# Lightning attention with a balanced expert layer: eight routing steps with the experts run beside them

## The chip, the core and the metric

One core of a Trainium2 chip runs the kernel alone. Its engines are TensorE (PE in the profile, with its weight loads listed apart as PEld), VectorE (DVE), ScalarE (ACT), GpSimd (POOL) and SyncE (SP). Each has its own queue of instructions and works through it in order; they wait for each other through semaphores. DMA transfers are issued from the queues of SP, ACT and POOL. The metric is the device time of one execution in microseconds, as the median of several runs. One execution was also profiled; every duration below is from it.

## What is computed

The input is a decayed linear attention over 4 batches, 8 heads, 768 positions and head size 64, in blocks of 64 positions:

```python
for b in range(nb):
    intra = np.einsum('bhic,bhjc->bhij', qb, kb) * Dmask[None]
    intra = np.einsum('bhij,bhjd->bhid', intra, vb)
    inter = np.einsum('bhid,bhde->bhie', qb * lam_pow[None], kv_state)
    out[:, :, sl] = intra + inter
    kv_state = lam_block[...] * kv_state + np.einsum('bhsd,bhse->bhde', kb_dec, vb)
```

Its output, seen as 3072 tokens of 512 numbers, goes through a layer of 8 experts. Every expert takes exactly 384 tokens. All 3072 x 8 scores are sorted, and the pairs are handed out from the best down:

```python
logits = x @ w_gate
order = np.argsort(-logits.flatten())
for idx in order:
    tok, e = (int(idx) // E, int(idx) % E)
    if assigned[tok] >= 0 or counts[e] >= cap:
        continue
    assigned[tok] = e
    counts[e] += 1
for e in range(E):
    mask = assigned == e
    out[mask] = np.maximum(x[mask] @ w1[e], 0.0) @ w2[e]
```

The assignment can be had without a sort. As long as no expert is full, every token goes to its best expert. At some score the first expert becomes full. From there on each remaining token's best choice is among the experts left, until the next one is full, and so on: eight fillings, each with one threshold.

## The kernel before

**Attention** (lines 146 to 286). For each batch, every head's q, k and v (192 KB each) are loaded, scaled, split into a high and a low bf16 part, and transposed on PE. Then six blocks of 128 positions follow, each over eight heads. The outputs are cast into `x_sb` (L285) and the gate scores into `logits_sb` (L286); one 3 MB transfer (L288) writes x to `x_dram` after the last batch.

**Weights** (L298, L300). All sixteen expert matrices are loaded by POOL's queue, from fp32 to bf16, right after attention. They take 16 buffers, so nothing depends on the routing.

**Routing.** Twelve rounds of a search for the first threshold (L345 to L358): DVE compares all scores with three candidates, reduces, and PE adds over the partitions. Tokens above the threshold are assigned. The rest are compacted to at most 640 rows by 120 one-hot matrices of 128x128 in fp32 (L426, L428). Seven phases (from L446) then fill the remaining experts: each takes every row's best open expert, sends the keys by a small DMA to one partition (L466), spreads them by PE (L468), ranks all against all (L473, L476), finds the worst score that still fits, and updates the state. After the last phase the assignment is scattered (L542), read back, turned into target positions, and a list of tokens by expert is scattered with 24 indirect DMAs (L587).

**Experts** (from L597), 0 to 7 in the order of their numbers. For each: load its token list `permt`, gather its 384 rows by three indirect DMAs `xe` (L606), transpose twelve tiles (L613) which ACT copies out one by one (L614), 32 matmuls with `w1t` (L619), relu on ACT (L621), 24 matmuls with `w2t` (L625), a copy on DVE (L628), and three indirect DMAs that scatter the rows to the output (L629). Their order by time follows a scheduler that places instructions into the queues by its own estimate of when they can run; what depends on nothing moves ahead.

What touches the change: `x_sb` and L288, everything from L298 to L587, and the expert loop.

Of the kernel before, what the change touches and what calls it, by code (L numbers as in the profile page):

```python
# [8 lines left out]

FP32 = mybir.dt.float32  # L10
BF16 = mybir.dt.bfloat16
I32 = mybir.dt.int32
AX = mybir.AxisListType
OP = mybir.AluOpType
# [3 lines left out]

# [3 lines left out]
def _PBF(a, lead):  # L22
    newap = [[0, lead[0]]] + [[0, r] for r in lead[1:]] + [list(x) for x in a.ap[1:]]
    return _dc.replace(a, ap=newap)


def _PBS(a, shape):
    newap = [[0, shape[0]]] + [[0, r] for r in shape[1:]]
    return _dc.replace(a, ap=newap)


@with_exitstack
def kernel(
# [11 lines left out]
    nc = tc.nc  # L45
    P = 128
# [5 lines left out]
    FF = 1024  # L52
    CAP = N // E
    NCHUNK = N // P
    NC = 5
    NEG = -64.0
# [3 lines left out]
    persist = ctx.enter_context(tc.tile_pool(name="persist", bufs=1))  # L60
    actx = ExitStack()
# [13 lines left out]

    slt = const.tile([P, P], BF16)
    nc.gpsimd.memset(slt, 0.0)
    nc.gpsimd.affine_select(
        out=slt, in_=slt, compare_op=OP.is_ge, fill=1.0, base=0,
        pattern=[[-1, P]], channel_multiplier=1,  # L80
    )

    ident = const.tile([P, P], FP32)
    make_identity(nc, ident)
    identb = const.tile([P, P], BF16)
    make_identity(nc, identb)

    ones_col = const.tile([P, 1], FP32)
    nc.vector.memset(ones_col, 1.0)
    ones128 = const.tile([P, P], FP32)  # L90
    nc.vector.memset(ones128, 1.0)
    ones_1 = const.tile([1, P], FP32)
    nc.vector.memset(ones_1, 1.0)

# [4 lines left out]

    iota_e_i = const.tile([P, E], I32)  # L100
    nc.gpsimd.iota(iota_e_i, pattern=[[1, E]], base=0, channel_multiplier=0)
    iota_e = const.tile([P, E], FP32)
    nc.vector.tensor_copy(iota_e, iota_e_i)
    iota3_i = const.tile([P, 3], I32)
    nc.gpsimd.iota(iota3_i, pattern=[[1, 3]], base=1, channel_multiplier=0)
    iota3 = const.tile([P, 3], FP32)
    nc.vector.tensor_copy(iota3, iota3_i)
    iotaU_i = const.tile([P, P], I32)
    nc.gpsimd.iota(iotaU_i, pattern=[[1, P]], base=0, channel_multiplier=0)
    iotaU = const.tile([P, P], FP32)  # L110
    nc.vector.tensor_copy(iotaU, iotaU_i)

    tok_i = const.tile([P, NCHUNK], I32)
    nc.gpsimd.iota(tok_i, pattern=[[P, NCHUNK]], base=0, channel_multiplier=1)
    row_i = const.tile([P, NCHUNK], I32)
    nc.gpsimd.iota(row_i, pattern=[[1, NCHUNK]], base=0, channel_multiplier=NCHUNK)
    row_f = const.tile([P, NCHUNK], FP32)
    nc.vector.tensor_copy(row_f, row_i)


# [16 lines left out]

    x_sb = persist.tile([P, NCHUNK, DM], BF16)
    logits_sb = persist.tile([P, NCHUNK, E], FP32)

    x_dram = dram.tile([N, DM], BF16)
    cdram = dram.tile([NC * P, 16], FP32)
    perm_dram = dram.tile([N, 1], I32)
    asgn_dram = dram.tile([N, 1], FP32)

    for b in range(B):
# [92 lines left out]
        for t in range(NB):  # L239
# [45 lines left out]
            nc.scalar.copy(x_sb[:, oc, :], po)  # L285
# [5 lines left out]
    wpre = ctx.enter_context(tc.tile_pool(name="wpre", bufs=1))  # L291
    w1r = moe_w1.rearrange("e (ko p) f -> e p ko f", p=P)
    w2r = moe_w2.rearrange("e (ko p) f -> e p ko f", p=P)
    w1ts = []
    w2ts = []
    for e in range(E):
        w1t = wpre.tile([P, 4, FF], BF16, tag=f"w1t{e}")
        nc.gpsimd.dma_start(out=w1t, in_=w1r[e])  # L298
        w2t = wpre.tile([P, 8, DM], BF16, tag=f"w2t{e}")
        nc.gpsimd.dma_start(out=w2t, in_=w2r[e])  # L300
        w1ts.append(w1t)
        w2ts.append(w2t)

    bctx = ExitStack()
    ap = bctx.enter_context(tc.tile_pool(name="ap", bufs=1))
    app = bctx.enter_context(tc.tile_pool(name="app", bufs=2))
    apps = bctx.enter_context(tc.tile_pool(name="apps", bufs=2, space=bass.MemoryType.PSUM))

    assigned = ap.tile([P, NCHUNK], FP32)
    nc.vector.memset(assigned, -1.0)  # L310
    counts = ap.tile([P, E], FP32)
    nc.vector.memset(counts, 0.0)
    capt = ap.tile([P, E], FP32)
    nc.vector.memset(capt, float(CAP))

    val0 = ap.tile([P, NCHUNK], FP32)
    nc.vector.reduce_max(val0, logits_sb, axis=AX.X)
    bsel0 = ap.tile([P, NCHUNK, E], FP32)
    nc.vector.tensor_tensor(bsel0, logits_sb, val0[:, :, None].to_broadcast([P, NCHUNK, E]),
                            OP.is_equal)  # L320
    cand0 = ap.tile([P, E, NCHUNK], FP32)
    c0v = cand0.rearrange("p e c -> p c e")
    nc.vector.tensor_tensor(c0v, logits_sb, bsel0, OP.mult)
    bm0 = ap.tile([P, NCHUNK, E], FP32)
    nc.vector.tensor_scalar(bm0, bsel0, 1.0, -NEG, OP.subtract, OP.mult)
    nc.vector.tensor_tensor(c0v, c0v, bm0, OP.add)

    npart = app.tile([P, E], FP32, tag="npart")
    nc.vector.reduce_sum(npart, bsel0.rearrange("p c e -> p e c"), axis=AX.X)
    nps = apps.tile([P, E], FP32, tag="aps1")  # L330
    nc.tensor.matmul(nps, ones128, npart, start=True, stop=True)
    ne = ap.tile([P, E], FP32)
    nc.vector.tensor_copy(ne, nps)

    lo = ap.tile([P, E], FP32)
    nc.vector.memset(lo, -0.625)
    mid = ap.tile([P, 3, E], FP32)
    step = 0.3125
    nc.vector.scalar_tensor_tensor(
        mid, iota3[:, :, None].to_broadcast([P, 3, E]), step,  # L340
        lo[:, None, :].to_broadcast([P, 3, E]), OP.mult, OP.add)
    capt3 = capt[:, None, :].to_broadcast([P, 3, E])
    for it in range(12):
        ge = app.tile([P, 3, E, NCHUNK], FP32, tag="ge")
        nc.vector.tensor_tensor(ge, cand0[:, None, :, :].to_broadcast([P, 3, E, NCHUNK]),  # L345
                                mid[:, :, :, None].to_broadcast([P, 3, E, NCHUNK]), OP.is_ge)
        gred = app.tile([P, 3, E], FP32, tag="gred")
        nc.vector.reduce_sum(gred, ge, axis=AX.X)
        cps = apps.tile([P, 3 * E], FP32, tag="aps1")
        nc.tensor.matmul(cps, ones128, gred.rearrange("p i e -> p (i e)"),  # L350
                         start=True, stop=True)
        sel = app.tile([P, 3, E], FP32, tag="sel")
        nc.vector.tensor_tensor(sel, cps.rearrange("p (i e) -> p i e", e=E), capt3, OP.is_ge)
        svec = app.tile([P, E], FP32, tag="svec")
        nc.vector.reduce_sum(svec, sel.rearrange("p i e -> p e i"), axis=AX.X)
        nc.vector.scalar_tensor_tensor(lo, svec, step, lo, OP.mult, OP.add)
# [305 lines left out]
```

## Time and profile before

| | us |
|---|---|
| median of 3 runs | 870.17 |
| fastest and slowest run | 861.41, 871.03 |
| profiled execution, first to last instruction | 862.5 |
| attention in it, up to | 393 |
| last w2 matmul of the last expert starts its block at | 845.82 |

The page gives no other time for the profiled execution than its span. On the page a row of a group says: line, engine, operation, what it writes and reads with the tile names (buffer numbers left out), the shape, how often; then the busy time of all, the mean of one in ns; then the engine's idle time ahead of them and what ended it. A row of the timeline says: start, duration, engine, line, operation, tiles, count, and in brackets the idle time ahead of it. A row of stretches is explained where it is shown. The granted clock is the share of its full clock at which PE was let run.

### The profile page before, as it was taken

The page shows a single profiled execution, that of the slowest core. Times are in us where ns is not written, and L with a number is a line of the kernel's source. Part 1 is how long each engine was busy: PE and PEld are TensorE (multiplying, and loading weights), DVE is VectorE, ACT ScalarE, POOL GpSimd, SP SyncE. Part 2 cuts the span into 40 slices and gives each one's busy share as a digit, 9 for nine tenths or more (in the row PEclk, how much of TensorE's full clock was granted, in tenths as well). Part 3 has the DMA queues.
Part 4 walks back from the last instruction along what each step waited for, and adds up shares of the span by engine and source line. Part 5 has one row for each costly group of instructions (what it writes and reads, how often), then busy time and mean ns, then how long its engine had stood idle before and what let it go on. Part 6 is the DMA issues. An engine that isn't in the chain of part 4 may idle for free. (4 is left out here: it accounts for less than half of the span.)

```text
span 862.5 us, 12438 instructions
## 1 busy us (share of the span) xinstructions
PE 544.2 (63%) x4353; PEld 452.3 (52%) x4353; DVE 416.8 (48%) x1722; ACT 208.1 (24%) x571; POOL 296.2 (34%) x679
## 2 busy tenths in 40 slices
PE   2799968997799978993169932232210003978774
PEld 1689957997689957993169921111100001434332
DVE  6754486545854477446665677667721000110101
ACT  4552245323542245220000000000000001444331
POOL 6822495228913496324110000000022333233342
PEclk9995556655555558555555555555555555988988
DMA  8400162005400170007999500000000001122121
GB/s 147 94 19 2 33 142 48 2 2 111 102 11 1 26 141 20 2 1 197 209 210 209 103 1 0 1 0 1 1 1 0 0 0 37 48 75 80 56 86 62
DMA packets 98078, 49.12 MB, mean 57 GB/s; under 512 B 80352, under 2 KB 91616, under 8 KB 98016
## 3 DMA queue, kind: packets, MB, share of 16 engines
q0 software_dynamic: 16544, 26.24, 14.2%
q1 hardware_dynamic: 56240, 15.80, 8.6%
q10 hardware_dynamic: 25232, 6.31, 3.4%
q8 instruction: 34, 0.56, 0.3%
q14 instruction: 28, 0.23, 0.1%
HBM read 55.62 MB, written 9.46 MB: 75 GB/s over the span
## 5 line engine op out<-in xcount | busy, mean ns | idle before, releaser
L614 ACT COPY xeT<-pt 128x128 bf16<-128x128 bf16 x96 | 18.4, 285 | 380.2 <-PE pt L613 379.6
L276 PE MATMUL pkv<-vgf,ksq 128*128 128x8 f32 x384 | 107.4, 354 | 0.0
L628 DVE COPY oe<-ph 128x512 f32<-128x512 f32 x24 | 16.6, 691 | 185.3 <-PE ph L625 146.6
L267 PE MATMUL pg<-vgf,sTm 128*128 128x8 f32 x384 | 104.9, 347 | 0.5 <-DVE sTm L257 0.5
L276 PEld LDWEIGHTS pkv<-vgf,ksq 128*128 128x128 f32 x384 | 98.8, 316 | 0.0
L267 PEld LDWEIGHTS pg<-vgf,sTm 128*128 128x128 f32 x384 | 94.9, 305 | 1.1 <-DVE sTm L257 0.8
L279 DVE TENSOR_TENSOR kvb_h<-kvb_h,pkv 64x64 bf16<-64x64 bf16 x192 | 40.8, 213 | 108.5 <-PE pkv L276 108.1
L281 POOL CAST kvg_h<-wg_acc 64x8 bf16<-64x8 f32 x192 | 37.9, 197 | 145.3 <-DVE lacc L271 77.2
L259 ACT CAST sTh<-sTm 128x128 bf16<-128x128 f32 x192 | 53.5, 298 | 113.6 <-DVE sTm L257 102.1
L613 PE MATMUL pt<-identb,xe 128*128 128x128 bf16 x96 | 11.2, 239 | 97.4 <-DMA xe<-x_dram,permt 95.5
L542 POOL DMA_INDIRECT asgn_dram<-asgc,tokci x5 | 5.0, 1001 | 189.4 <-DVE logc L530 183.7
L257 DVE TENSOR_TENSOR sTm<-ps,tri 128x128 f32<-128x128 f32 x192 | 52.2, 279 | 18.6 <-PE ps L254 15.4
L613 PEld LDWEIGHTS <-xe 128*128 128x128 bf16 x96 | 6.4, 104 | 104.0 <-issue 80.5
L428 PE MATMUL psC<-pay,pch 128*128 128x12 f32 x240 | 59.2, 373 | 2.5 <-DVE pch L426 2.5
L428 PEld LDWEIGHTS psC<-pay,pch 128*128 128x128 f32 x240 | 55.7, 311 | 6.1 <-DVE pch L426 2.6
L254 PE MATMUL ps<-TCh,TBh 128*128 128x128 bf16 x192 | 57.2, 301 | 0.0
L253 PE MATMUL ps<-TAh,TBh 128*128 128x128 bf16 x192 | 50.3, 265 | 7.3 <-ACT TBh L203 6.2
L619 PE MATMUL ph<-xeT,w1t 128*128 128x384 bf16 x256 | 54.3, 372 | 1.0 <-ACT xeT L614 0.9
L268 PEld LDWEIGHTS <-TAh 128*128 128x128 bf16 x192 | 53.1, 276 | 0.0
L274 PE MATMUL pkv<-vt,kt 128*128 128x64 bf16 x192 | 46.2, 241 | 7.8 <-DVE wg_acc L280 7.8
L426 DVE TENSOR_TENSOR pch<-pos,iou 128x128 f32<-128x128 f32 x120 | 35.0, 292 | 23.6 <-PE psC L428 16.0
L282 POOL TENSOR_TENSOR kvg_h<-wg_acc,kvg_h 64x8 bf16<-64x8 f32 x192 | 39.6, 206 | 14.9 <-POOL kvg_h L281 0.2
(233 smaller groups left out, 1468.5 us busy)
## 6 DMA issues: line engine op xcount, KB each, us to landing
w1t<-in_moe_w_dram POOLq DMA_DIRECT2D x8, 1024.0 KB
w2t<-in_moe_w_dram POOLq DMA_DIRECT2D x8, 1024.0 KB
vf<-in_v_dram ACTq DMA_DIRECT2D x32, 192.0 KB, 3.1
ksq<-in_q_dram SPq DMA_DIRECT2D x32, 192.0 KB, 3.6
kf<-in_k_dram SPq DMA_DIRECT2D x32, 192.0 KB, 2.9
x_dram<-x_sb SPq DMA_DIRECT2D x1, 3072.0 KB, 16.6
perm_dram<-tok_i,desti POOLq DMA_INDIRECT x24
xe<-x_dram,permt POOLq DMA_INDIRECT x24
```

Of the source, the lines that this page charges most:

```text
L253: nc.tensor.matmul(ps, TB, TA, start=True, stop=False)
L254: nc.tensor.matmul(ps, TB, TC, start=False, stop=True)
L257: nc.vector.tensor_tensor(sTm, ps, tri, OP.mult)
L259: nc.scalar.copy(sTh, sTm)
L267: nc.tensor.matmul(pg, sTm, vgf[:, t, :], start=True, stop=False)
L268: nc.tensor.matmul(pg, TA, kvg[h][:, 0, :], start=False, stop=False)
L274: nc.tensor.matmul(pkv[:, 0:D], kt[:, t, :, :], vt[:, t, 0, :], start=True, stop=False)
L276: nc.tensor.matmul(pkv[:, D : D + E], ksqs[h][:, t, :, :], vgf[:, t, :], start=False, stop=True)
L279: nc.vector.tensor_tensor(kvb[h][0:64], kvb[h][0:64], pkv[0:64, 0:D], OP.add)
L282: nc.gpsimd.tensor_tensor(kvg[h][0:64, 1, :], wgacc[h], kvg[h][0:64, 0, :], OP.subtract)
L428: nc.tensor.matmul(psC[:, uc, :], pch, pay[:, tci, :], start=(tci == 0), stop=(tci == NCHUNK - 1))
L619: nc.tensor.matmul(ph1, w1t[:, kc, fc * P : (fc + 1) * P], xeT[:, kc, :], start=(kc == 0), stop=(kc == 3))
```

## The change

Attention stays as it is but for its output: each block of 128 tokens is written to `x_dram` as soon as it is there, by 24 transfers on SP's queue.

Routing is new. `phase1` finds the first threshold with three counts instead of a search. A score is written as a number of three digits of seven bits each. For one digit, a one-hot-like matrix `ind` (is the token's digit at least k, for k = 0 to 127) is the stationary operand and the one-hot of the token's best expert the moving one; 24 bf16 matmuls give, for every k and every expert, how many tokens reach it. PE and a maximum turn this into the digit at which the first expert holds 384. After three digits the threshold is known. The tokens of every expert above it get slots by a prefix sum, and one more product gives the token list `perm` of the full expert. The rest of the tokens (at most 640) are compacted into 5 columns with keys `Z`.

`phase(i)` does the same for the remaining rows, with 5 matmuls per digit, and returns the list of the i-th expert to become full, and that expert's number. The eighth phase takes what is left and needs no count.

The experts run in the order in which they become full. After a phase, POOL reads the expert's number into a register, issues the loads of that expert's two matrices (three buffers now, where there were eight), and the gathers. Phase i + 1 is written ahead of expert i, so the scheduler may put them side by side. The copy of the output is now on ACT, and one copy takes four transposed tiles.

A flag collects the cases that this way can't handle: two equal scores of a token's best, more than 640 tokens left, counts that don't come out at 384. All engines read it at the end; if it is set, `_exact_path` does the whole routing over by bisection, with loops, and runs all experts again. Counting with the reference's own inputs, 260 tokens are left after the first filling.

The core of the diff, with the new functions:

```diff
+    def phase1(self, ctx, L):
...
+        def count(zq, onesm):
+            ind = sp.tile([P, P, 24], BF16, tag="ind", bufs=2)
+            cps = ps.tile([P, 8], F32, tag="cnt")
+            for hh in range(2):
+                ts = slice(hh * 12, hh * 12 + 12)
+                nc.vector.tensor_tensor(ind[:, :, ts], zq[:, None, ts].to_broadcast([P, P, 12]),
+                                        self.i_kt[:, :, ts], OP.is_ge)
+                for t in range(hh * 12, hh * 12 + 12):
+                    nc.tensor.matmul(cps, ind[:, :, t], ohb[:, t, :], start=(t == 0),
+                                     stop=(t == 23))
+            S = sp.tile([P, 8], BF16, tag="S", bufs=2)
+            nc.vector.tensor_scalar(S, cps, 384.0, None, OP.is_ge)
+            nps = ps.tile([P, 8], F32, tag="n")
+            nc.tensor.matmul(nps, onesm, S, start=True, stop=True)
+            nm = sp.tile([P, 1], F32, tag="nm", bufs=2)
+            nc.vector.reduce_max(nm, nps, axis=AX.X)
+            return nps, nm
...
+        for t in range(24):
+            nc.tensor.matmul(pe1, A[:, :, t], B1v[:, :, :, t], start=(t == 0), stop=(t == 23))
...
+        yield perm, eidx
...
+        for j in range(5):
+            nc.vector.tensor_tensor(
+                R[:, 87 + 24 * j : 87 + 24 * j + 24, :],
+                R[:, 58 + j : 59 + j, :].to_broadcast([P, 24, 24]),
+                Ls.rearrange("p s e t -> p (s e) t"), OP.mult)
+        psC = ps.tile([P, 207], F32, tag="pos")
+        for t in range(24):
+            nc.tensor.matmul(psC, A[:, :, t], R[:, :, t], start=(t == 0), stop=(t == 23))
...
+    def phase(self, i):
...
+            for r in range(3):
+                ind = sp.tile([P, 5, P], BF16, tag="indc")
+                cps = ps.tile([P, 8], F32, tag="cnt")
+                for c in range(5):
+                    nc.vector.tensor_scalar(ind[:, c, :], self.kio[r], zr[:, c : c + 1], None,
+                                            OP.is_le)
+                    nc.tensor.matmul(cps, ind[:, c, :], oh[:, c, :], start=(c == 0), stop=(c == 4))
+                S = sp.tile([P, 8], BF16, tag="Sc")
+                nc.vector.tensor_tensor(S, cps, self.big, OP.is_ge)
+                nps = ps.tile([P, 8], F32, tag="n")
+                nc.tensor.matmul(nps, self.ones[r], S, start=True, stop=True)
...
+        for c in range(5):
+            nc.vector.tensor_scalar(A5[:, c, :], self.kio1, kb[:, c : c + 1], None,
+                                    OP.is_equal)
+            nc.tensor.matmul(pe, A5[:, c, :], Bv[:, :, :, c], start=(c == 0), stop=(c == 4))
...
+class _Moe:
...
+        self.wp = ctx.enter_context(tc.tile_pool(name="mw", bufs=3))
...
+    def weights(self, eidx):
+        nc, P = self.nc, 128
+        ev = nc.values_load(eidx, engines=[mybir.EngineType.Pool], min_val=0, max_val=7)
+        return self.weights_at(ev)
+
+    def weights_at(self, ev):
+        nc, P = self.nc, 128
+        w1t = self.wp.tile([P, 4, 1024], BF16, tag="w1t")
+        nc.gpsimd.dma_start(out=w1t, in_=self.w1r[bass.ds(ev, 1)].rearrange("o p k f -> p (o k) f"))
+        w2t = self.wp.tile([P, 8, 512], BF16, tag="w2t")
+        nc.gpsimd.dma_start(out=w2t, in_=self.w2r[bass.ds(ev, 1)].rearrange("o p k f -> p (o k) f"))
+        return w1t, w2t
...
+            oe = self.mp.tile([P, 512], F32, tag="oe", bufs=4)
+            nc.scalar.copy(oe, p2)
+            nc.gpsimd.indirect_dma_start(
+                out=self.out, out_offset=bass.IndirectOffsetOnAxis(ap=perm[:, c : c + 1], axis=0),
+                in_=oe, in_offset=None, bounds_check=3071, oob_is_err=False)
...
+def _route_and_moe(ctx, tc, L, router, moe):
+    gen = router.phase1(ctx, L)
+    perm, eidx = next(gen)
+    xe = moe.gather(perm)
+    w1t, w2t = moe.weights(eidx)
+    for _ in gen:
+        pass
+    for i in range(8):
+        if i < 7:
+            nperm, neidx = router.phase(i + 1)
+            nxe = moe.gather(nperm)
+            nw = moe.weights(neidx)
+        moe.ffn(perm, xe, w1t, w2t)
+        if i < 7:
+            perm, xe, (w1t, w2t) = nperm, nxe, nw
+    return router.flag()
+
+def _check_and_mend(ctx, tc, L, router, moe, dram, fi):
+    fv = tc.nc.values_load(fi, min_val=0, max_val=1)
+    with tc.If(fv > 0):
+        with ExitStack() as fctx:
+            _exact_path(fctx, tc, L, router, moe, dram)
...
-            nc.scalar.copy(x_sb[:, oc, :], po)
+            xs = work.tile([P, DM], BF16, tag="xs")
+            nc.scalar.copy(xs, po)
+            nc.sync.dma_start(out=x_dram[oc * P : (oc + 1) * P, :], in_=xs)
             nc.gpsimd.tensor_copy(logits_sb[:, oc, :], lacc)
-
-    nc.sync.dma_start(out=x_dram.rearrange("(c p) d -> p c d", p=P), in_=x_sb)
     actx.close()
...
-    for e in range(E):
-        w1t = wpre.tile([P, 4, FF], BF16, tag=f"w1t{e}")
-        nc.gpsimd.dma_start(out=w1t, in_=w1r[e])
-        w2t = wpre.tile([P, 8, DM], BF16, tag=f"w2t{e}")
-        nc.gpsimd.dma_start(out=w2t, in_=w2r[e])
...
-    for ph in range(7):
...
+    moe = _Moe(ctx, tc, identb, x_dram, moe_w1, moe_w2, out)
+    fi = _route_and_moe(ctx, tc, logits_sb, router, moe)
+    _check_and_mend(ctx, tc, logits_sb, router, moe, dram, fi)
```

How the scheduler lays this out, at two places. First PE, between two experts. Before, an expert is transposes and then its w1 matmuls, with nothing between (`xe` the gathered rows, `pt` their transposes, `ph` the first product):

```order
L613 LDWEIGHTS xe
L613 MATMUL pt<-identb,xe 128x128
L613 LDWEIGHTS xe
L613 MATMUL pt<-identb,xe 128x128
L619 LDWEIGHTS w1t
L619 MATMUL ph_8580<-xeT,w1t 128x384
```

In the new kernel, at the start of the expert after the second one: the last matmul of a count (`cps`, from the indicators `ind` and the one-hots `oh`), a tile's four transposes, and then the matmul that turns the count into a digit (`nps`, from `S`).

```order
L330 LDWEIGHTS ind
L330 MATMUL cps<-oh,ind 128x8
L483 LDWEIGHTS xe
L483 MATMUL pt<-identb,xe 128x128
L483 LDWEIGHTS xe
L483 MATMUL pt<-identb,xe 128x128
L483 LDWEIGHTS xe
L483 MATMUL pt<-identb,xe 128x128
L483 LDWEIGHTS xe
L483 MATMUL pt<-identb,xe 128x128
L334 LDWEIGHTS ones_95
L334 MATMUL nps<-S,ones_95 128x8
```

The three counts of the next phase now stand between this expert's transposes and its first w1 matmuls; the later products of the phase stand between w1 matmuls, and the 24 w2 matmuls stay in one piece.

Second POOL. Before, its queue in the expert stage holds gathers and scatters alone, after the two scatters of the routing:

```order
L542 DMA asgn_dram<-asgc,tokci 3072x1 x5
L587 DMA perm_dram<-tok_i,desti 3072x1 x24
L606 DMA xe<-x_dram,permt 128x512 x6
L629 DMA out_dram<-oe,permt 3072x512 x3
L606 DMA xe<-x_dram,permt 128x512 x3
```

In the new kernel a step is the read of the expert's number (`ei`), the two weight loads, the gathers with the new list, and the scatters of the expert before:

```order
L466 TENSOR_LOAD ei
L466 ISA x2
L472 ISA
L472 DMA w1t<-in_moe_w_dram 128x4x1024
L474 ISA
L474 DMA w2t<-in_moe_w_dram 128x8x512
L458 DMA xe<-x_dram,perm 128x512 x3
L500 DMA out_dram<-oe,perm 3072x512 x3
```

So the weights moved from ahead of the routing to the middle of each step, and each scatter of an expert now stands between the gathers of one phase and the register read of the next.

More of the change, by code (lines that the diff above doesn't have):

```diff
@@ L60 @@
     persist = ctx.enter_context(tc.tile_pool(name="persist", bufs=1))
+    ident = const.tile([P, P], FP32)
+    make_identity(nc, ident)
+    identb = const.tile([P, P], BF16)
+    make_identity(nc, identb)
+    router = _Router(ctx, tc, ident, identb)
+    logits_sb = persist.tile([P, NCHUNK, E], FP32)
+    x_dram = dram.tile([N, DM], BF16)
     actx = ExitStack()
@@ L98 @@
     nc.vector.tensor_copy(n_idx, n_idx_i)
[L100 to L118, printed above, removed]
     lam_sb = const.tile([P, E], FP32)
@@ L136 @@
     nc.vector.tensor_tensor(wg_lo[0:64], wgf, wg_hi[0:64], OP.subtract)
[L138 to L144, printed above, removed]
     for b in range(B):
@@ L307 @@
[L307 to L356, printed above, removed]
-        step = step * 0.25
-        nc.vector.scalar_tensor_tensor(
-            mid, iota3[:, :, None].to_broadcast([P, 3, E]), step,
-            lo[:, None, :].to_broadcast([P, 3, E]), OP.mult, OP.add)
```

858 lines of the change are left out of this document (561 added, 297 removed).

## The prediction

> **What bounds the kernel now.** I read first the busy time by stretches, with the stage borders taken from the timeline, then the groups by line, then the timeline at the borders. (The page's chain of waits holds only the last three pieces and says nothing of the stages.) Columns: stretch in us, length, busy time and instructions of PE, PE's weight loads, DVE, ACT, POOL, granted clock, DMA share, GB/s.
>
> ```profile
> 0.00:393.00 393.00, 334.81 (x3452) 315.05 (x3452) 231.11 (x1142) 158.17 (x411) 206.03 (x581) 0.62 0.24 50
> 393.00:434.00 41.00, 8.80 (x32) 7.38 (x31) 29.29 (x85) 0.13 (x1) 12.83 (x19) 0.50 1.11 227
> 434.00:496.00 62.00, 57.29 (x233) 53.89 (x233) 38.46 (x147) 0.00 (x0) 2.52 (x3) 0.50 0.98 172
> 496.00:625.00 129.00, 33.79 (x85) 20.86 (x84) 91.75 (x294) 0.00 (x0) 0.00 (x0) 0.50 0.01 0
> 625.00:722.00 97.00, 2.88 (x10) 2.15 (x10) 9.55 (x34) 0.00 (x0) 28.40 (x30) 0.50 0.01 0
> 722.00:862.50 140.50, 106.64 (x544) 52.96 (x544) 16.59 (x24) 49.81 (x160) 46.43 (x48) 0.88 0.20 68
> ```
>
> Attention takes 393 us. The next 329 us are routing: threshold search (41), compaction by fp32 matmuls (62), seven phases (about 129), scatters (97). In each of these one engine, or one small transfer, works while the rest wait. Then come 140.5 us of experts, with PE busy for 106.64. Two groups show what the long stretches consist of:
>
> ```profile
> L473 DVE TENSOR_TENSOR gr<-k1b,key 128x3200 f32<-128x3200 f32 x7 | 24.4, 3492 | 0.2
> ...
> L587 POOL DMA_INDIRECT perm_dram<-tok_i,desti x24 | 23.3, 972 | 51.9 <-DMA perm_dram<-tok_i,desti 42.6 <-DVE desti L585 9.3
> ```
>
> The change deletes all of that and puts most of the experts inside what remains of the routing. So the time after is: end of attention, first filling, six steps that each hold one routing phase and one expert, two more experts, tail.
>
> **Attention (kept, with two edits).** The new first routing instruction on DVE waits for POOL's last logits copy and, because its tile lies where the x pieces lay, for the x transfers.
>
> ```profile
> 392.54 0.59 ACT L285 CAST x_sb<-po 128x512 bf16<-128x512 f32 x1 [1.25 <-PE po L263]
> ...
> 394.62 0.15 DVE L280 TENSOR_TENSOR wg_acc<-wg_acc,pkv 64x8 f32<-64x8 f32 x1
> ...
> vf<-in_v_dram ACTq DMA_DIRECT2D x32, 192.0 KB, 3.1
> ```
>
> Last cast done at 393.1, 0.4 to issue, some 3 us for a 128 KB piece (192 KB takes 3.1): 396.6. The 24 pieces stand in SP's queue ahead of later q and k loads; at a batch border those wait for the old buffers anyway, so I cost them at nothing. The new POOL constants stand ahead of POOL's first attention work:
>
> ```profile
> 5.22 0.91 POOL L189 TENSOR_TENSOR vt<-vf,vt 128x384 bf16<-128x384 f32 x1 [2.12 <-ACT vt L188]
> ...
> 10.80 2.11 POOL L172 TENSOR_TENSOR ksq<-kf,lamneg 128x384 f32<-128x384 f32 x2 [3.50 <-ACT lamneg L161]
> ...
> L109 POOL IOTA iotaU_i<- 128x128 int32 x1 | 0.2, 224 | 0.0
> L96 POOL IOTA n_idx_i<- 128x6 int32 x1 | 0.1, 123 | 0.0
> ```
>
> (224 - 123)/122 = 0.83 ns an element; 4,700 elements are 3.9 us, against 5.6 us that POOL idles there. I take +1. Attention's end: 397.5 (395 if DVE is not held, 402 with the constants uncovered).
>
> **First filling.** The prices of a short DVE instruction, of a DVE-PE-DVE trip, and of two-byte data:
>
> ```profile
> 521.02 0.17 DVE L491 TENSOR_TENSOR sfxB<-sfxA 128x8 f32<-128x8 f32 x1
> 521.22 0.17 DVE L491 TENSOR_TENSOR sfxA<-sfxB 128x8 f32<-128x8 f32 x1
> ...
> 536.10 0.22 DVE L533 TENSOR_REDUCE nfp<-buc 128x8 f32<-128x40 f32 x1
> ...
> 536.37 0.60 PE L535 MATMUL dps<-nfp,ones 128*128 128x8 f32 x2 [1.24 <-DVE nfp L533]
> 537.00 0.17 DVE L536 TENSOR_TENSOR counts<-counts,dps 128x8 f32<-128x8 f32 x1 [0.58 <-PE dps L535]
> ...
> L270 PEld LDWEIGHTS <-TCh 128*128 128x128 bf16 x192 | 20.2, 105 | 0.0
> L201 DVE COPY TAh<-TAp 128x768 bf16<-128x768 bf16 x32 | 17.7, 553 | 10.5 <-PE TAp L196 10.3
> ```
>
> A dependent short instruction costs 0.20, a trip 0.68 in fp32 and about 0.35 with one bf16 pass. A half indicator has 1,536 elements: 1.7 us by L473 (1.09 ns an element), 1.1 by L201 (0.72). I take 1.2, near the bf16 row. Normalising: 16 instructions and two trips, 4.6. Each of three counts: two halves 2.4, twelve pairs left at 0.11, two trips 0.7, three short instructions 0.6: 5.0, so 15. From the threshold to the token list: 9.3 (two halves of A, 24 pairs half hidden, one trip, some 16 short ones). Compaction: five products 2.5, 24 matmuls of 207 columns 4.3, 0.3. Keys: 14 instructions, 3.0. Sum 39. The second phase's first count stands behind the first expert's transposes and four matmuls, hence behind its gather and weights, due at about 40: 42 in all. Ends: 33 (halves at 0.8, independent short instructions at 0.1), 52 (halves at 1.7, and 6 us of waits).
>
> **Six steps.** PE's prices per expert, at full and at half clock (the stretch row shows 0.50 there, after some 4 us of little work):
>
> ```profile
> 743.00 5.65 PE L619 MATMUL ph<-xeT,w1t 128*128 128x384 bf16 x32
> ...
> 748.49 5.34 PE L625 MATMUL ph<-w2t,hT 128*128 128x512 bf16 x24
> ...
> 757.24 7.10 PE L619 MATMUL ph<-xeT,w1t 128*128 128x384 bf16 x32 [0.19 <-ACT xeT L614]
> ...
> 758.15 0.15 PEld L619 LDWEIGHTS <-w1t 128*128 128x128 bf16 x1 [0.17 <-issue]
> ...
> 758.00:760.00 2.00, 2.00 (x8) 0.91 (x6) 0.69 (x1) 0.50 (x2) 0.97 (x1) 0.50 0.00 0
> ```
>
> In PE's new order the count rounds stand between transposes, the rest of the phase between w1 matmuls, and w2 follows whole. Routing chain: a round is five indicators at 0.2, two trips and three short instructions, 2.3; three make 6.9, with 0.4 ahead 7.3. Then 14 instructions to the selection (2.0), a trip (0.7), 17 more (2.5), a trip and two (0.8): 6.0. PE does the transposes and about six w1 matmuls in the rounds; the other 26, ten at 0.32 and sixteen at 0.18, take 6.1 beside the 6.0. Then 0.5 for the last relu and 5.34 for w2, with a few tenths per handover: 20.
>
> [...]
>
> POOL's prices, and the weights' rate:
>
> ```profile
> 751.37 0.99 POOL L606 DMA_INDIRECT xe<-x_dram,permt  x1 [4.63 <-DMA permt<-perm_dram]
> ...
> 752.66 0.96 POOL L606 DMA_INDIRECT xe<-x_dram,permt  x1 [0.30 <-issue]
> ...
> 852.50 0.96 POOL L629 DMA_INDIRECT out_dram<-oe,permt  x1 [2.52 <-DMA out_dram<-oe,permt]
> 855.97 0.96 POOL L629 DMA_INDIRECT out_dram<-oe,permt  x1 [2.51 <-issue]
> ...
> 397.58 0.94 POOL L300 DMA_DIRECT2D w2t<-in_moe_w_dram  x1
> 398.50 0.78 POOL L298 DMA_DIRECT2D w1t<-in_moe_w_dram  x1
> ...
> 420.00:430.00 10.00, 1.77 (x6) 1.50 (x6) 7.12 (x19) 0.00 (x0) 1.64 (x2) 0.50 1.18 209
> ...
> w1t<-in_moe_w_dram POOLq DMA_DIRECT2D x8, 1024.0 KB
> ...
> permt<-perm_dram SPq DMA_DIRECT2D x8, 1.5 KB, 1.6
> ```
>
> Two matrices, 2.1 MB, at 209 GB/s: 10 us. POOL in a step, from the moment the expert is known: reading its number (no row; 0 to 1.6, the landing of the smallest load; I take 1.0, nearer that load than nothing), two weight issues 1.7, three gathers at 1.27 once the token list is there (6.0 later): 9.8. Behind that first read wait the step's weights, its gathers and the previous expert's scatters, and PE waits for the first two. Then three scatters, each waiting for the one before (3.47 apart). I assume that their data stands behind the 10 us of weights, as all are issued by POOL; so the first lands near 16.5 and the last is issued near 21.5. That is a little over PE's 20, and each gather is due just as the weights end. I take 22.5 a step: 135. Ends: 19 (clock up, scatters not held) and 28 (half clock: 7.3 + 8.3 + 0.5 + 10.2 + 1.5). ACT takes DVE's output copies: it was busy 49.81 of 140.5 us there, and the 24 copies add some 0.6 each, so I cost them at nothing. SP's loads of keys and of token lists go; nothing stood behind them.
>
> **Last two experts and tail.** Phase eight has no count. Two experts at 2 + 6.5 + 5.34 and a hand-over: 29 (27 to 34). Before, the end follows the last w2 by 862.5 - 851.2:
>
> ```profile
> 845.82 5.34 PE L625 MATMUL ph<-w2t,hT 128*128 128x512 bf16 x24
> ```
>
> That is 11.3; reading the flag and jumping over the general path has no row (0 to 6; I take 2): 13.3.
>
> **Sum.** 397.5 + 42 + 135 + 29 + 13.3 = 617 against a span of 862.5, 245 less. The three runs stand from 1 below to 8.5 above that span (median 870.17), so I add 4: 621. Ends: 580 and 674, with the 4, 584 and 678.
>
> **Rivals.**
>
> POOL slowed by DVE. Routing's DVE work now runs beside POOL's issues, as it did not in 722:862.5. The trace has POOL held by DVE:
>
> ```profile
> 393.90 0.19 POOL L281 CAST kvg_h<-wg_acc 64x8 bf16<-64x8 f32 x1 [0.55 <-DVE wg_acc L280]
> ...
> 394.90 0.53 POOL L281 CAST kvg_h<-wg_acc 64x8 bf16<-64x8 f32 x1 [0.54 <-DVE wg_acc L280]
> ...
> 394.69 0.61 DVE L323 TENSOR_TENSOR cand<-logits_sb,bsel 128x192 f32<-128x192 f32 x1
> ```
>
> 0.53 in place of 0.19, 2.8 times. If that befell all eight issues of a step, 8 x 0.96 x 1.8 = 14 us more on POOL; if half of them, 7: 28.5 a step, 657. Against it: the weight issues at 397 to 399 took 0.78 and 0.94 beside DVE work.
> [...]
>
> Cheaper routing: two-byte DVE work at half price and PE mostly at full clock. First filling 35, steps 18.5: 397.5 + 35 + 111 + 29 + 13.3 = 586, 590 with the 4. For it: the mean granted clock of the expert stretch was 0.88.
>
> No overlap: each expert waits for its weights, which are asked for only once the phase names it. 1 + 1.7 + 10 + 2 = 15 from name to arrival, then 11 of matmuls, after 7.8: 34 a step, 686, with the 4, 690. Against it: the weights of expert i+1 are asked for while expert i runs, and there are three buffers.
>
> The other side: the flag is up and the general path runs. Its eight passes of 161 halvings have some 15 DVE instructions and a trip each, about 3.8 us: 4.9 ms more, slower by far. It decides when over 640 tokens are left after the first filling, or two keys tie at a border. From the reference's inputs I count 260 left and no tie among the borders, though the chip's logits differ in the last bits.
>
> **Chances.** Forecast (steps of 20.5 to 25) 0.62; POOL slowed 0.14; cheaper 0.14; no overlap 0.07; flag 0.03. Predicted 621. The range reaches over the slowed case and down to the lower sum: 584 to 690; what lies beyond is most of the last two. Only the flag makes it slower, and nothing of weight lies within 2% (about what a measurement of this kernel can tell from no change): faster 0.96, same 0.01, slower 0.03.
>
> **What would show it.** Right: the first count of phase two starts some 42 us after attention, successive first counts stand 22 to 23 us apart, w2 blocks take 5.3 to 7, POOL is nearly never idle in a step, and gathers land just ahead of the transposes. Wrong: PE waiting for w1t or xe in every step (no overlap), POOL's issues well over 1 us (slowed), steps under 20 with POOL idle (cheaper), or instructions of lines 584 to 700 in the trace (flag).

## The result, and the profile after

| | before | after |
|---|---|---|
| median of 4 runs, us | 868.47 | 630.46 |
| fastest and slowest, us | 861.41, 871.03 | 628.56, 632.08 |
| profiled execution, span, us | 862.5 | 629.6 |

The ratio is 0.7265, with a 95% interval of 0.7231 to 0.7300. The forecast was 621 (584 to 690): the direction and the range hold, the time came 9.5 us later.

Busy time by stretches of the changed kernel, with borders at its own stages (columns as in the prediction):

```profile
404.00:424.00 20.00, 8.06 (x82) 6.36 (x81) 14.16 (x53) 0.89 (x2) 1.52 (x4) 0.50 0.00 0
424.00:447.00 23.00, 15.07 (x74) 8.11 (x75) 10.69 (x47) 2.36 (x5) 5.12 (x5) 0.50 0.60 109
447.00:460.00 13.00, 11.42 (x82) 5.67 (x81) 9.37 (x66) 5.19 (x10) 3.87 (x4) 0.95 0.37 57
460.00:484.00 24.00, 15.49 (x92) 8.52 (x94) 7.47 (x57) 6.85 (x13) 8.91 (x9) 0.72 0.84 171
484.00:500.00 16.00, 14.16 (x108) 7.91 (x107) 8.40 (x62) 7.63 (x15) 3.78 (x5) 1.00 0.44 103
500.00:522.50 22.50, 7.07 (x40) 4.12 (x41) 4.93 (x35) 3.52 (x7) 7.07 (x8) 0.56 0.72 151
522.50:545.90 23.40, 16.16 (x101) 8.81 (x101) 8.36 (x61) 7.43 (x14) 7.88 (x9) 0.79 0.70 141
545.90:569.30 23.40, 15.97 (x109) 8.97 (x109) 8.74 (x66) 7.55 (x15) 7.85 (x8) 0.75 0.68 141
569.30:596.00 26.70, 23.60 (x131) 12.27 (x132) 6.84 (x55) 10.93 (x21) 12.76 (x13) 0.87 0.92 171
596.00:610.00 14.00, 11.62 (x66) 5.91 (x64) 0.00 (x0) 7.34 (x14) 1.97 (x2) 1.00 0.59 124
610.00:629.60 19.60, 0.07 (x1) 0.00 (x0) 0.00 (x0) 0.58 (x1) 3.91 (x4) 0.64 0.15 57
```

The two rows of 23.40 are steps in their steady form, and in them nothing is full: PE is busy for 16 of 23.4 us, DVE for 8, POOL for 8, and the DMA engines for 0.7. A step that no engine and no transfer fills is a chain of waits. The row 484 to 500 is a step that got its rows in time: 16 us with PE busy for 14. Its gathers were issued from 475.98 on, ahead of their step's second matrix (479.64), and landed in 2.8 us each. The last row, 19.6 us, holds next to nothing.

Three lines of the waits from 436 us to the end (who waited for whom: sum, times, longest) show where the chains run:

```profile
POOL out_dram L500 <- DMA out_dram<-oe,perm: 35.0, 7, 9.6
...
DVE nm L336 <- PE nps L334: 32.0, 18, 14.6
PE pt L483 <- DMA xe<-x_dram,perm: 32.0, 5, 14.1
```

PE's transposes wait 32 us in all for the gathered rows, DVE waits just as long, most of it for matmuls of the routing that stand behind these transposes, and POOL waits 35 us for scatters to land. One step, from one w1t issue to the next, from the timeline of the changed kernel:

```profile
522.48 0.81 POOL L472 DMA_DIRECT2D w1t<-in_moe_w_dram  x1 [2.07 <-DVE Z L404]
...
530.12 0.99 POOL L458 DMA_INDIRECT xe<-x_dram,perm  x1 [0.30 <-issue]
531.42 1.04 POOL L500 DMA_INDIRECT out_dram<-oe,perm  x1 [0.31 <-issue]
...
537.20 0.50 PE L483 MATMUL pt<-identb,xe 128*128 128x128 bf16 x3 [5.44 <-DMA xe<-x_dram,perm]
...
539.25 1.00 POOL L500 DMA_INDIRECT out_dram<-oe,perm  x1 [6.79 <-ACT xeT L484]
542.78 0.98 POOL L500 DMA_INDIRECT out_dram<-oe,perm  x1 [2.53 <-DMA out_dram<-oe,perm]
...
543.57 0.23 DVE L341 TENSOR_SCALAR E<-nps,nm 128x8 f32<-128x8 f32 x1
...
544.12 0.13 DVE L309 TENSOR_SCALAR ei<-ef 1x1 int32<-1x1 f32 x1
...
545.88 0.81 POOL L472 DMA_DIRECT2D w1t<-in_moe_w_dram  x1 [2.13 <-DVE Z L404]
```

Two chains lead from the first line to the last. By the rows: the weights are asked for at 522.48, the rows arrive behind them at 537.2 (14.7 later), the transposes and the next phase's three counts take until 543.57 (6.4), the expert's number is there at 544.25 and POOL has read it at 545.88 (0.7 and 1.6). By the scatters: the first is issued at 531.42, the second only when the first has landed behind the weights, the third again 3.5 later, so POOL is free at 543.76. The chains end 0.5 us apart. (The releaser that is named at 539.25, a copy of transposes on ACT, is nothing that a scatter needs; the first scatter landed 7.0 us after its issue, at 538.4, and the wait is for that.) Which of them sets the step can't be read from this trace; the experiments ask that.

The last part of the timeline, with the last expert's w2 and the last two of the scatters behind it:

```profile
604.73 1.46 PE L496 MATMUL p<-w2t,hT 128*128 128x512 bf16 x5
605.81 4.26 PE L496 MATMUL p<-w2t,hT 128*128 128x512 bf16 x19
...
620.15 0.98 POOL L500 DMA_INDIRECT out_dram<-oe,perm  x1 [2.50 <-issue]
623.64 0.98 POOL L500 DMA_INDIRECT out_dram<-oe,perm  x1 [2.51 <-issue]
```

### The profile page after: what moved, and what is told of

Same layout as the page of the kernel before. It is cut to its first block, busy times and chain, and to the rows that moved or that the text cites. A ratio compares the mean times of both kernels' runs of the same rounds, so it can differ in the third digit from the quotient of the medians.

```text
span 629.6 us, 12329 instructions
## 1 busy us (share of the span) xinstructions
PE 485.4 (77%) x4331; PEld 403.1 (64%) x4339; DVE 312.5 (50%) x1628; ACT 218.7 (35%) x526; POOL 275.7 (44%) x654
## 3 DMA queue, kind: packets, MB, share of 16 engines
q1 hardware_dynamic: 54304, 15.75, 11.2%
## 5 line engine op out<-in xcount | busy, mean ns | idle before, releaser
L890 PE MATMUL pg<-vgf,sTm 128*128 128x8 f32 x384 | 108.1, 356 | 0.0
L890 PEld LDWEIGHTS pg<-vgf,sTm 128*128 128x128 f32 x384 | 98.7, 317 | 0.1
L489 PE MATMUL p<-xeT,w1t 128*128 128x384 bf16 x256 | 60.5, 384 | 4.8 <-ACT xeT L484 4.8
L500 POOL DMA_INDIRECT out_dram<-oe,perm x24 | 24.1, 1002 | 83.0 <-DMA out_dram<-oe,perm 35.0
L884 PE MATMUL po<-vt,sTh 128*128 128x64 bf16 x192 | 45.3, 245 | 0.0
L496 PE MATMUL p<-w2t,hT 128*128 128x512 bf16 x184 | 42.9, 379 | 0.4
L492 ACT ACTIVATE hT<-p 128x384 bf16<-128x384 f32 x64 | 31.4, 490 | 33.8 <-PE p L489 29.5
L484 ACT COPY xeT<-pt 128x512 bf16<-128x512 bf16 x24 | 14.1, 586 | 81.8 <-PE pt L483 66.9
L886 PE MATMUL po<-kvb_h,TAh 128*128 128x64 bf16 x192 | 41.5, 226 | 0.0
L489 PEld LDWEIGHTS <-w1t 128*128 128x128 bf16 x256 | 26.6, 112 | 22.8 <-issue 15.7
## 6 DMA issues: line engine op xcount, KB each, us to landing
w2t<-in_moe_w_dram POOLq DMA_DIRECT2D x8, 1024.0 KB, 13.3
```

What stands on the lines that cost most here:

```text
L489: nc.tensor.matmul(p1, w1t[:, kc, fc * P : (fc + 1) * P], xeT[:, kc].rearrange("p c s -> p (c s)"), start=(kc == 0), stop=(kc == 3))
L496: nc.tensor.matmul(p2, hT[:, kc, c * P : (c + 1) * P], w2t[:, kc, :], start=(kc == 0), stop=(kc == 7))
L884: nc.tensor.matmul(po[:, h * D : (h + 1) * D], sTh, vt[:, t, 0, :], start=True, stop=False)
L886: nc.tensor.matmul(po[:, h * D : (h + 1) * D], TA, kvb[h], start=False, stop=True)
L890: nc.tensor.matmul(pg, sTm, vgf[:, t, :], start=True, stop=False)
```

## The experiments

The theories that the expectations speak of: **L**, the loop over four engines by the gathered rows; **S**, POOL's queue with its scatters that wait for one another; **T**, both, closing at the same time; the rest are told where they occur. Steps are read between w1t issues.

**Scatters that do not wait.** The eight experts' rows are different rows of the output, so a scatter need not wait for the one before.

```diff
+        self.scatters = []
...
-            nc.gpsimd.indirect_dma_start(
+            sc = nc.gpsimd.indirect_dma_start(
...
+            if free:
+                for o in self.scatters:
+                    self.tc.declare_no_dep(sc.ins, o, reason="rows differ")
+                self.scatters.append(sc.ins)
...
-        moe.ffn(perm, xe, w1t, w2t)
+        moe.ffn(perm, xe, w1t, w2t, free=True)
```

> Scatters of the experts' rows no longer wait for one another (their rows differ); all else as in the changed kernel, whose steady step from one w1t issue to the next is 23.4 us (522.48, 545.88, 569.34). Theory L (a loop over four engines: w1t issue, gathered rows land behind the weights 14.7 later, transposes and the next phase's three counts 6.4, the expert's number 0.6, POOL's read of it 1.7): the step stays at 23 to 23.5, only the tail shrinks (19.5 us from the last w2 matmul to the end become 10 to 13), total 616 to 622. Theory S (POOL's queue sets the step, because the second and third scatter wait for the one before, whose data stand behind the weights): the step falls to PE's 20, total 598 to 606.

Measured: 613.86 (611.61 to 620.76), below what L expected and above S. POOL's timeline of this run (its lines stand one further down):

```profile
533.07 0.82 POOL L473 DMA_DIRECT2D w1t<-in_moe_w_dram  x1 [11.31 <-DVE Z L404]
...
544.51 0.98 POOL L501 DMA_INDIRECT out_dram<-oe,perm  x1 [0.30 <-issue]
...
557.01 0.82 POOL L473 DMA_DIRECT2D w1t<-in_moe_w_dram  x1 [11.52 <-DVE scr L351]
...
604.15 0.98 POOL L501 DMA_INDIRECT out_dram<-oe,perm  x1 [0.74 <-ACT oe L500]
```

POOL now issues all three scatters at once and then stands idle for 11.5 us, until the expert's number comes. The last three steps are 22.7, 23.0 and 23.9: S alone does not set them. Most of what was gained lies at the end: the last w2 block ends at 603.2 and the span at 610.5, so the tail is 7.3 instead of 19.5.

**Two phases ahead.** Phase i + 2 is written ahead of expert i; the buffers of `xe` and `perm` grow by one.

```diff
+    todo = [(perm, xe, w1t, w2t)]
     for i in range(8):
-        if i < 7:
-            nperm, neidx = router.phase(i + 1)
+        while len(todo) < 3 and i + len(todo) < 8:
+            nperm, neidx = router.phase(i + len(todo))
             nxe = moe.gather(nperm)
             nw = moe.weights(neidx)
-        moe.ffn(perm, xe, w1t, w2t)
-        if i < 7:
-            perm, xe, (w1t, w2t) = nperm, nxe, nw
+            todo.append((nperm, nxe) + nw)
+        moe.ffn(*todo.pop(0))
```

> Phase i + 2 is written ahead of expert i (before: phase i + 1), so a phase's counts stand behind the transposes of an expert whose rows were asked for a whole step earlier. Scatters wait for one another as before. Theory L: PE no longer waits for xe (32 us in all before) and the step falls to PE's 20 (18 to 21), total 606 to 616. Theory S: the step stays at 23 to 24, total 626 to 634. If both chains close at the same time (T), this run and the one with free scatters each gain little in the step, and only both together bring 20.

Measured: 619.32 (614.97 to 619.86), between what L and S expected. POOL's timeline:

```profile
507.93 1.03 POOL L500 DMA_INDIRECT out_dram<-oe,perm  x1 [0.57 <-ACT oe L499]
518.35 1.00 POOL L500 DMA_INDIRECT out_dram<-oe,perm  x1 [9.39 <-ACT hT L492]
521.90 0.98 POOL L500 DMA_INDIRECT out_dram<-oe,perm  x1 [2.55 <-DMA out_dram<-oe,perm]
522.94 0.80 POOL L472 DMA_DIRECT2D w1t<-in_moe_w_dram  x1
```

The number of the expert that is asked for at 522.94 was known at 514.09 (the end of its instruction on DVE). For 8.9 us its issue stood behind scatters that wait for one another. PE's wait for `xe` is down to 5.5 us, in one place, and the other chain took over.

**Both.**

> Two phases ahead and free scatters together. Theory L: as the run with two phases ahead, less the tail's 6 to 9: 596 to 608. Theory S: as the run with free scatters alone, 598 to 606. Theory T (two chains that tie): steps of 18 to 20 here alone, and a total at least 10 below each single edit.

Measured: 588.74 (586.95 to 593.00), 25 below the one and 31 below the other; the ratio to the kernel before is 0.6778 (0.6723 to 0.6832). POOL's timeline:

```profile
489.60 0.81 POOL L473 DMA_DIRECT2D w1t<-in_moe_w_dram  x1 [1.75 <-DVE Z L404]
...
506.95 0.80 POOL L473 DMA_DIRECT2D w1t<-in_moe_w_dram  x1 [3.51 <-DVE jb L378]
...
524.30 0.82 POOL L473 DMA_DIRECT2D w1t<-in_moe_w_dram  x1 [6.99 <-DVE scr L351]
```

Two steps of 17.35. To leave attention's variation out, count from the first routing instruction on DVE (404.69, 400.19, 403.33 and 398.37 in the four profiles, in the order named next) to the end of the span: 224.9 in the changed kernel, 210.3 with free scatters, 214.5 two ahead, 187.5 with both. The single edits gain 14.6 and 10.4, together 37.4: more than their sum. These sums still hold the tail, which free scatters shorten as well. From the second expert's w2 block to the seventh's, five steps, the four profiles take 111.3, 108.9, 101.2 and 84.4: in the steps alone the single edits gain 2.4 and 10.1, together 26.9. That is T, two chains that tie. Its expected 18 to 20 was a little high, since PE's time without waits is below 20 (see the run with three matrices).

**x written at once.** `x_sb` and its one transfer come back.

```diff
+    x_sb = persist.tile([P, NCHUNK, DM], BF16)
...
-            xs = work.tile([P, DM], BF16, tag="xs")
-            nc.scalar.copy(xs, po)
-            nc.sync.dma_start(out=x_dram[oc * P : (oc + 1) * P, :], in_=xs)
+            nc.scalar.copy(x_sb[:, oc, :], po)
...
+    nc.sync.dma_start(out=x_dram.rearrange("(c p) d -> p c d", p=P), in_=x_sb)
```

> x is kept in on-chip memory and written by one 3 MB transfer after attention, as in the kernel before; the constants of the routing stay where they are on POOL. Theory Q (the 24 small x writes on SP's queue hold back the next batch's q and k loads): attention's last VectorE instruction goes from 403.7 back to 395 to 398, total 622 to 626. Theory K (the 5.5 us of constants on POOL ahead of attention's first work): attention still ends at 402 to 404, total 628 to 632.

Measured: 630.83 (625.84 to 634.97), no change in the median, where Q expected 622 to 626. The one profile can't tell Q from K: the last cast of x stood at 397.7 here, and at 401.6, 397.0, 400.3 and 395.4 in the four kernels whose attention is the same. So the 9 us by which attention ended later than in the first profile of the kernel before may be no effect of the change at all.

**The kernel before, once more.**

> The kernel before, unchanged, in another execution. If attention's end varies between executions (R), its last cast of x stands not at 392.5 as in the first profile but up to some 8 us later, as in the four kernels with 24 x writes, where it stood at 395.4, 397.0, 400.3 and 401.6. If the change itself made attention longer (A), it stands at 392 to 394 again.

Measured: 869.7, span 867.9. The last cast of x, in this execution and in the changed kernel's:

```profile
398.39 0.59 ACT L285 CAST x_sb<-po 128x512 bf16<-128x512 f32 x1 [1.25 <-PE po L263]
```

```profile
401.60 0.58 ACT L909 CAST xs<-po 128x512 bf16<-128x512 f32 x1 [1.25 <-PE po L886]
```

In the kernel before it stands 5.9 later than in that kernel's first profile (392.54). R holds: attention's end varies by some 6 us between executions of one kernel, and the first profile was a short one. An effect of the change of a few us can't be told apart from that.

**Gathers ahead of the weights,** with free scatters.

```diff
     xe = moe.gather(perm)
-    w1t, w2t = moe.weights(eidx)
+    with tc.issue_after(moe.last_gather.ins):
+        w1t, w2t = moe.weights(eidx)
...
             nxe = moe.gather(nperm)
-            nw = moe.weights(neidx)
...
+            with tc.issue_after(moe.last_gather.ins):
+                nw = moe.weights(neidx)
```

> Free scatters as in the run of that name (613.9), and POOL issues the three gathers ahead of the read of the expert's number and the weights. Theory L (the rows land late because they stand behind the weights in POOL's one queue): the last gather lands 2.5 to 4 us after its issue instead of 8, PE no longer waits for xe, but w1t is now asked for some 9 us later and PE waits for it: the step is w1t's landing 8.9, some 5 of w1 matmuls up to the next token list, gathers 4, read and issue 2.5: 20 to 21, total 596 to 606. Rival E (they land late because the DMA engines are full, whatever the order): the last gather still takes 7 us or more, and the step grows to 24 or more, total 615 to 630.

Measured: 605.80 (604.69 to 608.56). The gathers' line of the page's part on DMA issues, with free scatters alone and here (the last number is the median of us to landing):

```profile
xe<-x_dram,perm POOLq DMA_INDIRECT x24, 8.9
```

```profile
xe<-x_dram,perm POOLq DMA_INDIRECT x24, 2.8
```

The gathers read the same rows in both, the scatters are free in both, and only the order of the issues differs: the landing goes from 8.9 (8.3 in the changed kernel) to 2.8. E, by which it stays at 7 or more whatever the order, falls. Yet in the steady steps here the gathers are issued when the weights of the step before have landed, so this run alone doesn't tell a queue that is served in order from DMA engines that are busy. The changed kernel's trace speaks for the queue: in the step shown above w2t landed at 536.8, the three gathers issued 4 to 7 us behind it at 537.2, 537.5 and 537.8, and the scatter behind them at 538.4, all in the order of their issues. The steps are 21.4 and 20.9 (w1t at 497.18, 518.57, 539.43), near the 20 to 21 that the loop by way of w1t gives, and PE waits 24.8 us for w1t instead.

**Three matrices in turn.**

```diff
+    fixed = [moe.weights_at(i) for i in range(3)]
...
-    w1t, w2t = moe.weights(eidx)
+    w1t, w2t = fixed[0]
...
-            nw = moe.weights(neidx)
+            nw = fixed[(i + 1) % 3]
...
-    _check_and_mend(ctx, tc, logits_sb, router, moe, dram, fi)
```

> Left out: the loading of each expert's own weights and the flag with the general path. Three experts' matrices are loaded once after attention and used in turn, so a step holds no weight transfer and no read of a number; scatters wait for one another and phases stand one ahead as in the changed kernel. If the transfer of the weights inside the step is what stretches both chains (L and S): gathers and scatters land 3 us after issue, the step falls to PE's own time, 15 to 17, total 570 to 585. If the chain over PE and DVE alone needs the 20 us that were predicted for it (P): steps of 20, total 600 to 612.

Measured: 589.89 (587.20 to 593.15). The w2 blocks on PE's timeline:

```profile
507.51 5.34 PE L496 MATMUL p<-w2t,hT 128*128 128x512 bf16 x24
522.73 5.34 PE L496 MATMUL p<-w2t,hT 128*128 128x512 bf16 x24
539.01 5.34 PE L496 MATMUL p<-w2t,hT 128*128 128x512 bf16 x24
```

Steps of 15.2 and 16.3, as expected, with one phase ahead and chained scatters. The total lies 5 above the upper expected end; the second expert's step is 25 long (its w2 block begins at 476.0, the first expert's at 450.9). The trace shows most of why: that expert's token list came only at 457.9, after the first expert's w2, its gathers were issued at 460.96, behind a scatter that waited for the one before, PE's transposes began at 463.8, and until 476.0 the w1 matmuls ran in part at 0.48 each instead of 0.32. P, the forecast's 20, falls.

**No flag.** The call of `_check_and_mend` is left out.

> Left out: the reading of the flag and the general path. Forecast's term: the end comes 2 us (0 to 6) sooner after the last scatter, which in the changed kernel is issued at 623.64, 6.0 before the end. If the read costs nothing: 5.5 to 6.5 from the last scatter's issue to the end, as before (855.97 to 862.5).

Measured: 623.63; the last scatter is issued here, and the span ends at 622.0:

```profile
617.57 0.98 POOL L500 DMA_INDIRECT out_dram<-oe,perm  x1 [2.51 <-issue]
```

4.4 from issue to end, against 6.0 with the flag: about 1.5, near the forecast's 2. But the kernel before, which has no flag, took 6.5. So the price is small, and its size is not settled.

**All three edits** (two ahead, free scatters, gathers first), and **a third of the output** (two ahead, free scatters, `if free and c > 0: continue` ahead of the scatter).

> Two phases ahead, free scatters, and the gathers issued ahead of the read and the weights. With two phases ahead (588.7) rows and weights are asked for a step early, and the core's transfers are busy all through its steps (share 1.07 to 1.10 of the DMA engines, 227 to 240 GB/s). Theory D (the transfers' rate is the bound there): the order of gathers and weights changes nothing, 584 to 594. If the wait for rows still counts in it (L): 5 to 10 less, 578 to 584. If asking later for the weights counts: 595 to 605.

> Two phases ahead and free scatters, and only the first of each expert's three scatters is left: two thirds of the output are not written (0.5 MB less of some 3.3 MB a step). Theory D: steps of 17.35 (w1t issue 489.60, 506.95, 524.30) fall to 14 to 15.5. If PE and DVE set them (P: 15.8 in the run without weights in the steps): 16 to 17.5, no change.

Measured: 593.90 (590.93 to 596.22) and 587.00, the second in a single run. The order of gathers brings nothing more once rows are asked for a step early, as D has it. Of the second run, the w1t issues:

```profile
495.52 0.81 POOL L473 DMA_DIRECT2D w1t<-in_moe_w_dram  x1 [3.74 <-PE p L490]
511.36 0.81 POOL L473 DMA_DIRECT2D w1t<-in_moe_w_dram  x1 [7.28 <-DVE Z L404]
527.70 0.81 POOL L473 DMA_DIRECT2D w1t<-in_moe_w_dram  x1 [6.96 <-DVE scr L351]
```

Steps of 15.8 and 16.3, above D's 14 to 15.5 and at the lower edge of P's 16 to 17.5: with two thirds of the scatters gone the step stands where PE and DVE put it without weights (15.2 to 16.3). The five steps from the second expert's w2 block to the seventh's agree: 84.4 us with the whole output, 78.6 here, 78.9 with three matrices in turn. So the transfers' rate costs some 1 to 1.5 of the 17.35 us, the chain over PE and DVE stands right beneath it, and D as the only bound falls. The best version that computes the whole layer is the one with two phases ahead and free scatters, 588.74.

## Why the prediction was right, and where it was not

By its own sum, in the profiled execution (617 forecast, 629.6 measured):

| term | forecast | measured | from the rows |
|---|---|---|---|
| attention's end | 397.5 | 404.7 | first routing instruction on DVE, 404.69 |
| first filling | 42 | 39.6 | first count of phase two, 444.26 |
| six steps | 135 | 133.4 | end of the sixth expert's w2, 577.6 |
| last two experts | 29 | 32.4 | end of the last w2, 610.1 |
| tail | 13.3 | 19.5 | end of the span |

**Attention** was off by 7.2, mostly by how the profile was read: the 393.1 on which the term was built came from an execution whose attention was some 6 us shorter than in the second execution. The 4 us added for the medians covered a part of it. What the constants on POOL cost, forecast at 1, is lost in this variation.

**First filling.** Near in sum, by two errors that cancel. The timeline of the changed kernel:

```profile
409.64 0.95 DVE L150 TENSOR_TENSOR ind<-q,i_kt 128x1536 bf16<-128x1536 bf16 x1
...
420.69 0.17 DVE L160 TENSOR_REDUCE nm<-nps 128x1 f32<-128x8 f32 x1 [0.26 <-PE nps L158]
...
429.56 0.16 DVE L227 TENSOR_REDUCE perm<-pe 128x3 int32<-128x6 f32 x1 [1.10 <-PE pe L224]
...
431.66 8.98 PE L269 MATMUL psC<-R,A 128*128 128x207 bf16 x24 [2.13 <-DVE R L263]
```

A half indicator took 0.95, below the 1.2 taken, and the three counts 11.2 instead of 15. The token list came after 8.9 (forecast 9.3). The 24 matmuls of 207 columns took 8.98 instead of 4.3, 0.37 each: the stretch row shows a clock of 0.50 there.

**Six steps.** The sum is right, 133.4 for 135, and the parts are right on POOL: the last scatter was forecast to be issued near 21.5 after the expert is known, and it was issued at 21.9 (number there at 520.85, issue at 542.78). Two things were wrong. First, PE's 20 was too long. In the step at 484 the counts took 5.1 from the end of w2 (484.62) to the digit (489.67), where 7.3 stood, and the rest up to w2 4.6 (494.28), where 6.1 and 0.5 stood, with the clock at 1.00: 15 in all. (The upper end of a step, 28, holds 1.5 for TensorE's clock, a price per step that no run shows. What the trace shows in its place is the stretch from the first w1 matmul to w2: 6.24 us in the step at 484, at a granted clock of 1.00, and 8.64, from 541.08 to 549.72, at 0.65 on the mean in the step shown above, where PE had stood idle for 5.44 us ahead of its transposes.) Second, and this is the step of the forecast that failed: "each gather is due just as the weights end" was taken as no wait, and PE and POOL were treated as two queues of which the longer one sets the step. In truth the gather's landing stands in a loop with the next weights' issue, by PE's queue, since the counts of the next phase come behind transposes that need the rows. The loop is 23.4, and the scatters, 22.9 with the read, hide right behind it. That the sum was right owes something to this coincidence, and something to luck in the mean: the first of the six took 14.3 (444.26 to the end of its w2 at 458.6), with next to no waiting on PE, and the other five 23.8 each on the mean, with w2 blocks between 15.0 and 32.0 apart. The sign "22 to 23 us apart" did not show step by step.

**Last two experts and tail** were mis-sized by 3.4 and 6.2. The seventh expert's transposes had to wait for its rows, and its w1 matmuls took 8.16, where 6.5 had been put:

```profile
579.20 0.40 PE L483 MATMUL pt<-identb,xe 128*128 128x128 bf16 x4 [1.46 <-DMA xe<-x_dram,perm]
...
582.61 8.16 PE L489 MATMUL p<-xeT,w1t 128*128 128x384 bf16 x32 [0.64 <-ACT xeT L484]
```

For the tail the forecast took the kernel before, where scatters are 3.5 apart but none is late. Here the sixth expert's last scatter (594.32) landed only behind the eighth expert's weights, so the seventh's first could not be issued before 603.86, and four scatters, 3.5 apart, were issued after the last w2 matmul was done (the first at 613.20). With free scatters the tail is 7.3. (The forecast's upper ends add up to 673, not 674; nothing hangs on it.)

**The rivals.** POOL was not slowed by DVE as the rival had it; the 0.14 given to it was the author's estimate. A weight issue of the changed kernel, and the indicator-like instruction that began beside it:

```profile
454.85 0.95 POOL L474 DMA_DIRECT2D w2t<-in_moe_w_dram  x1
...
455.31 0.51 DVE L391 TENSOR_SCALAR A<-i_kp,kb 128x128 bf16<-128x128 bf16 x1
```

The issue takes 0.95, as in the kernel before (0.94), and it is DVE's instruction that takes 0.51 where its like takes 0.26 on the mean; POOL's issue had begun 0.46 us ahead of it. By kind, POOL's issues took 0.84, 0.96, 1.03 and 1.00 on the mean (w1t, w2t, gathers, scatters) against 0.80, 0.91, 0.97 and 0.97 before: 3 to 7% more, where the rival had up to 180%. "No overlap" was wrong as a price (34 a step), but its sign, PE waiting for `xe`, was there five times: the waiting was real, and PE's shorter work made room for it. "Cheaper routing" was right on PE's work in a step, 15 where 20 was forecast, and the loop ate the gain; the first filling stayed at 39.6, above its 35. The flag was not up.

## What to carry to other kernels

When a step takes longer than the work of any one engine in it, and nothing is full, look for a loop: follow one iteration from a request to the next request of the same kind, across engines, and add up. Two chains that end within half a microsecond of each other hide one another; an edit to one shows little, and only both together show what each is worth. Bulk loads and small gathers on one queue should be asked for in the order in which they are needed (here the gathers landed 8.3 us after their issue on the median where most stood behind the weights, and 2.8 with the gathers first), and a profile whose span stands at the edge of the runs' times should be looked at twice before a stage border is taken from it.

## What the runs showed of the hardware

On the median, a gather of 128 rows landed 2.8 us after its issue in the run with gathers first and 8.3 in the changed kernel, where most stand behind two matrices of 1 MB; a scatter of 128 rows landed after 12.2 in the run with gathers first, where most stand behind the step's weights, and after 2.8 with three matrices, where no weights move in the steps. With two phases ahead and free scatters, the core's transfers ran at 227 and 240 GB/s with a DMA share of 1.10 and 1.07, above the 209 of the weights alone in the kernel before. Attention alone, with nothing data-dependent in it, took 393.9 to 401.6 us to its last cast of x in nine kernels that share its code.
